# Scan of chunks 1 to 5 as one unit of four batches, with B and C turned on VectorE

## The chip, the core and the metric

The kernel runs on one core of one Trainium2 chip. The metric is the time of one execution on the device in microseconds (us), the median of three runs. PE is TensorE (matmuls), DVE VectorE, ACT ScalarE, POOL GpSimd, and SP SyncE, which issues all loads and stores here.

## The reference

A chunked state-space scan, then a gated feed-forward layer (FFN) over its result:

```python
# x (4, 8, 768, 32)   a (4, 8, 768)   B, C (4, 8, 768, 16): batch, head, token, ...
L = np.exp(cum[:, :, :, None] - cum[:, :, None, :]) * causal     # decays inside a chunk
M = np.einsum('bhin,bhjn->bhij', Cc, Bc) * L
y_intra = np.einsum('bhij,bhjd->bhid', M, xc)
y_inter = np.einsum('bhin,bhnd->bhid', Cc, state) * np.exp(cum)[:, :, :, None]
y[:, :, sl] = y_intra + y_inter
state = decay_full[:, :, None, None] * state + sum_over_j(B_j x_j decay_from_j)
...
x = y.transpose(0, 2, 1, 3).reshape(3072, 256)
out = (1 / (1 + np.exp(-(x @ w_gate))) * (x @ w_val)) @ w_out    # 256 -> 1536 -> 256
```

All in float32. The length of a chunk is free as long as the result is the same.

## The kernel before, in words

The kernel cuts the 768 tokens into six chunks of 128, each in two halves of 64. A chunk has four batches, so 512 rows of the FFN. The FFN of chunk k goes over twelve blocks f of 128 of the 1536 columns: a gate product `pg` and a value product `pv` each (L784, six matmuls, since an exact float32 product is made from a high and a low part of x and of w), sigmoid on ACT, the products h on DVE, ACT and POOL (L715 to L745), and then the projection `po` of each batch j = 0 to 3 over all f (L821, L822, and in chunk 0 L810). In chunk 0 the first six f are single products (L775). Chunk 0 has a scan of its own (FirstUnit). The scan of chunk c+1 is woven into the FFN of chunk c.

For chunks 1 to 5 a unit is one batch of one chunk, and two units make a pair. For one unit: `products` turns the loaded B and C (tokens on partitions) with two TensorE transposes `pt` (L393, L394); ACT copies the result to `bct` and masks C by group of heads (L404, L408). `multiply` makes C times B for a pair (L473). `decays` scans a into the decay matrix on DVE (L428) and makes `bd`, B times the last decay (L438); `before` makes `cd`, C times the running decay (L450). `results` is the rest of a pair: `weigh` (L487), `within` (L499 the part inside a chunk, L506 the state's increment), `ml` and the state in the middle of the chunk `sm` (L514, L541), `inter` (L550), the parts `xh` and `xl` of the result (L564, L570), and `state` makes `sn` (L460). So TensorE makes six visits to the scan per chunk (multiply, within, inter for two pairs) and four pairs of transposes.

The order of the instructions on each engine is set while the program is built, by a list scheduler. Each piece of work is a generator that yields one step after another:

```python
yield step("pe", 0.24 if c else 0.45, needs, [("tp", u)], **{hold: 1})
yield step("act", 0.9 if c else 1.1, [], [("bct", u)], **{hold: -1})
```

A step names the engine, a planned cost, what it needs and makes, and buffers that it takes or gives back. `run` picks, among the steps that could begin within 0.1 us of the first, the one whose task has the earliest due time; due times come from a formula by chunk (`unit`, L945), and the table `DUES` overrides them by task name. A planned time is only used to put the instructions in order. Loads are steps on "sp" with the planned cost of one issue and a planned time of transfer; SP issues its DMAs in that order, over eight lanes. Per chunk the loads are 8 of `ab` (L288, the decays, repeated over partitions from the scratch tensor `a_z`), 4 of `bn` and `cn` (L275), 2 of `xn` (L282) and 4 of `pp` (L296, from the scratch `a_p`). The two scratch tensors are written once (`save_z`, `save_p`, L895, L898) after `a` is clipped and its products are made (L883). A loaded weight tile is 512 KB; each of the 18 is clipped (L323), rounded and split into two parts over DVE, ACT and POOL (L330 to L353).

Of the kernel before, what the change touches and what calls it, by code (L numbers as in the profile page):

```python
# [37 lines left out]
LANES = 8  # L38
HOLD = 0.1
# [5 lines left out]
POOL_SB = 1.15  # L45
# [10 lines left out]
UNIT1_D = 7.0  # L56
FFN1 = 77.0
UNIT_T = 14.9
UNIT_D = 0.0
AHEAD = 46.7  # L60
STATE = 30.0
SPARE = 1.0
FILLS = {"products0_2": {0: 5}, "result0_1": {1: 2}, "result0_2": {1: 2}, "result0_3": {0: 3}}
# [6 lines left out]
def tile_ssd_then_gated_ffn(  # L70
# [25 lines left out]
    NDEC = 6  # L96
    NPRE = 5
# [82 lines left out]
    def run():  # L180
# [4 lines left out]
        landed = [0.0] * LANES  # L185

# [13 lines left out]
        while tasks:  # L200
# [30 lines left out]
            if eng == "sp":  # L231

                many, end = round(cost / 0.52), start
                for _ in range(many):
                    end = max(end, landed[-LANES]) + 0.52
                    dma_free = max(dma_free, end + DMA_L) + port / many
                    landed.append(dma_free + DMA_L)
            free[eng] = end
# [14 lines left out]
            try:  # L253
                t[2] = t[4].send(eng)
            except StopIteration:
# [8 lines left out]
    def pair_of(tag, c, b, shape):  # L264

        k = tag, c, b // 2
        if k not in got:
            got[k] = ld.tile([P, 2, H, shape], F32, tag=tag, name=f"{tag}{c}_{b // 2}", bufs=2)
        return got[k]

    def load_bc(c, b, n):
        cs = slice(c * L, (c + 1) * L)
        for tag, src in (("bn", b4), ("cn", c4)):
            t = pair_of(tag, c, b, N)
            nc.sync.dma_start(  # L275
                t[:, b % 2 : b % 2 + n].rearrange("p b h n -> p (b h) n"), src[cs, b * H : (b + n) * H]
            )

    def load_x(c, b, n):
        cs, hs, bs = slice(c * L, (c + 1) * L), slice(b * H, (b + n) * H), slice(b % 2, b % 2 + n)  # L280
        t = pair_of("xn", c, b, D)
        nc.sync.dma_start(t[:, bs].rearrange("p b h d -> p (b h) d"), x4[cs, hs])  # L282

    def load_a(c, b):
        t = ld.tile([P, H, L2], F32, tag="ab", name=f"ab{c}_{b}", bufs=NDEC)
        for i in range(2):
            src = a_z[2 * c + i, b * H : (b + 1) * H].rearrange("(o h) l -> o (h l)", o=1)
            nc.sync.dma_start(  # L288
                t[i * L2 : (i + 1) * L2].rearrange("p h l -> p (h l)"), src.broadcast_to([L2, H * L2])
            )  # L290
        got["a", c * NB + b] = t

    def load_p(c, b):
        t = ld.tile([P, L], F32, tag="pp", name=f"pp{c}_{b}", bufs=NPRE)
        src = a_p[b, :, c * L : (c + 1) * L].rearrange("h (o l) -> h o l", o=1).broadcast_to([H, N, L])
        nc.sync.dma_start(t, src)  # L296
        got["pp", c * NB + b] = t
# [18 lines left out]
    def split_w(i):  # L316
# [18 lines left out]
        yield step("pool", POOL_SB, [], [("whole", i)])  # L335
# [31 lines left out]
    units = {}  # L367
    states = {}

    def state_of(u, name):  # L370

        return wk.tile([P, NG * D], F32, tag=f"st{u % NB}", name=f"{name}{u}", bufs=3)

    class Unit:


        def __init__(self, c, b):
            self.c, self.b, self.u = c, b, c * NB + b
            self.nm = f"{c}_{b}"
            self.more = c < NCH - 1  # L380

        def products(self):

            c, b, u = self.c, self.b, self.u
            needs = [("bc", u)]
            if c:
                needs += [("bct", u - 1 if c > 1 else -1), ("cb", u - 4), ("cd", u - 4)]
            needs += [("x", 0, NB - 1)] if c == 1 else []
            pool, tag, hold = (ps_y, "py", "y") if c else (ps_mm, "mm", "banks")
            yield step("pe", 0.24 if c else 0.45, needs, [("tp", u)], **{hold: 1})  # L390
            bn, cn = (got[k, c, b // 2][:, b % 2].rearrange("p h n -> p (h n)") for k in ("bn", "cn"))
            pt = pool.tile([P, 512], F32, tag=tag, name=f"pt{self.nm}")
            nc.tensor.transpose(pt[:, :L], bn, eye)  # L393
            nc.tensor.transpose(pt[:, L : 2 * L], cn, eye)  # L394
            yield step("act", 0.9 if c else 1.1, [], [("bct", u)], **{hold: -1})
            if c:
                self.bct = wk.tile([P, 4, L], F32, tag="bct", name=f"bct{self.nm}", bufs=4)
            else:

                if ("bct", b // 2) not in got:  # L400
                    got["bct", b // 2] = hp.tile([P, 2, 4, L], F32, tag=f"h{b // 2}", name=f"bct{self.nm}")
                self.bct = got["bct", b // 2][:, b % 2]
            if c:
                nc.scalar.copy(self.bct[:, :2].rearrange("p k l -> p (k l)"), pt[:, : 2 * L])  # L404
            else:
                nc.scalar.copy(self.bct[:, 0], pt[:, :L])
            for g in range(NG):
                nc.scalar.mul(self.bct[:, 2 + g], pt[:, L : 2 * L], of_g[:, g : g + 1])  # L408
# [110 lines left out]
    def results(*two):  # L519
# [51 lines left out]
        if more:  # L571
# [3 lines left out]
            for k, t in enumerate(two):  # L575
                t.after = ml[:, k]
# [447 lines left out]
```

## Time and profile before

| what | value |
|---|---|
| the three runs | 378.0, 377.8, 377.15 us; median 377.8 us |
| span of the profiled execution | 375.7 us |
| its own time | not given apart; the runs lie 1.45 to 2.3 us above the span, the median 2.1 us |
| PE busy | 365.3 us, 97% of the span |
| DVE, ACT, POOL busy | 155.8, 151.2, 153.9 us, 41% each |
| the DMA engines | 26.27 MB, mean 70 GB/s |
| PE's last matmul ends | 372.4 us |

The span runs from the first to the last instruction of one execution. PE is the engine to follow: the others are busy for less than half the time, and what counts of them is when they make PE wait. "Granted clock" is the clock at which TensorE was allowed to run, 1.00 for 2.4 GHz and 0.50 for 1.2 GHz.

### The profile page before, as it was taken

What the parts mean: (1) busy time and instruction counts of PE and PEld (TensorE: products, weight loads), DVE (VectorE), ACT (ScalarE), POOL (GpSimd) and SP (SyncE); (2) the same over time, 40 slices, a digit from 0 to 9 for tenths busy, and PEclk for the clock granted to TensorE, in tenths of its full rate; (3) what the DMA queues carried; (4) which work ended last, traced back from release to release, by engine and by line L of the source; (5) the groups of instructions that cost most, each with busy time, mean ns of one, the idle gap of its engine ahead of it and who ended that gap; (6) DMA issues with size and microseconds to landing.
All of it is one profiled execution on the core that took longest, in us unless ns stands there. A gap on an engine that the chain in (4) does not pass through costs nothing.

```text
span 375.7 us, 8098 instructions
## 1 busy us (share of the span) xinstructions
PE 365.3 (97%) x3360; PEld 286.3 (76%) x3360; DVE 155.8 (41%) x280; ACT 151.2 (40%) x319; POOL 153.9 (41%) x161
## 2 busy tenths in 40 slices
PE   8879999989999999999999999999999999999996
PEld 2565478758788888887788888788877788888885
DVE  4774755854874234253431452550132440122201
ACT  2567578223536421436510435420335420244400
POOL 4346557573669540245430055430145420145410
PEclk9999999989999999999999999999999999999999
DMA  7998964087520043415502303120000000000000
GB/s 153 139 352 181 226 241 155 30 126 142 107 50 16 0 88 69 67 49 58 91 9 58 97 4 39 34 38 30 28 3 2 2 2 28 30 0 0 2 28 28
DMA packets 89270, 26.27 MB, mean 70 GB/s; under 512 B 76306, under 2 KB 82002, under 8 KB 89234
## 3 DMA queue, kind: packets, MB, share of 16 engines
q1 hardware_dynamic: 89234, 25.76, 30.7%
q8 instruction: 26, 0.43, 0.5%
q14 instruction: 10, 0.08, 0.1%
HBM read 22.41 MB, written 3.34 MB: 69 GB/s over the span
## 4 chain that ended last, share of the span: by engine, by line
PE 78%; SPq 12%; DMA 7%; issue 1%; DVE 1%; POOL 0%; DVEq 0%; POOLq 0%
PE pg L784 22%; PE pv L784 22%; PE po L821 15%; PE po L822 7%; SPq L275 4%; PE po L810 4%; DMA wr<-in_moe_w_gate_dram 3%; SPq L313 2%; PE pcb L499 2%; DMA a_z<-a 2%; SPq L309 2%; SPq L282 2%; SPq L288 2%; PE pcb L473 2%; DMA cn<-in_C_dram 2%; PE pcb L550 1%
## 5 line engine op out<-in xcount | busy, mean ns | idle before, releaser
L745 POOL TENSOR_TENSOR h<-g,h 128x512 fp32r<-128x512 f32 x60 | 79.0, 1316 | 124.6 <-ACT h L743 122.0
L784 PE MATMUL pg<-xh,w 128*128 128x512 f32 x264 | 93.8, 396 | 0.0
L784 PE MATMUL pv<-xh,w 128*128 128x512 f32 x264 | 93.7, 396 | 0.0
L821 PE MATMUL po<-w,h 128*128 128x512 f32 x228 | 81.8, 402 | 0.0
L739 DVE TENSOR_TENSOR g<-pv,g 128x512 f32<-128x512 f32 x60 | 41.4, 691 | 91.4 <-PE pv L784 86.6
L743 ACT CAST h<-g 128x512 fp32r<-128x512 f32 x60 | 37.3, 621 | 78.4 <-DVE g L739 78.4
L822 PE MATMUL po<-w,h 128*128 128x256 f32 x228 | 63.9, 280 | 0.0
L784 PEld LDWEIGHTS pg<-xh,w 128*128 128x128 f32 x264 | 49.5, 188 | 11.4 <-issue 0.5
L784 PEld LDWEIGHTS pv<-xh,w 128*128 128x128 f32 x264 | 49.6, 188 | 10.6 <-issue 0.2
L784 PE MATMUL pg<-xl,w 128*128 128x512 f32 x132 | 51.5, 390 | 0.0
L784 PE MATMUL pv<-xl,w 128*128 128x512 f32 x132 | 51.4, 390 | 0.0
L821 PEld LDWEIGHTS po<-w,h 128*128 128x128 f32 x228 | 42.8, 188 | 10.7 <-issue 0.2
L715 ACT ACTIVATE g<-pg 128x512 f32<-128x512 f32 x72 | 43.1, 599 | 19.4 <-PE pg L784 13.7
L822 PEld LDWEIGHTS po<-w,h 128*128 128x128 f32 x228 | 43.0, 189 | 0.2
L837 ACT COPY o<-po 128x256 f32<-128x256 f32 x20 | 7.5, 373 | 67.3 <-PE po L822 66.7
L839 DVE TENSOR_TENSOR o<-po,o 128x256 f32<-128x256 f32 x20 | 8.5, 425 | 59.8 <-ACT o L837 59.7
L353 POOL TENSOR_TENSOR w<-wr,w 128x512 fp32r<-128x512 f32 x18 | 24.7, 1371 | 14.2 <-ACT w L351 10.8
L428 DVE TENSOR_TENSOR_SCAN ab<-ab,delta 128x512 f32<-128x512 f32 x20 | 26.5, 1331 | 5.6 <-DMA ab<-a_z 5.6
L784 PEld LDWEIGHTS pv<-xl,w 128*128 128x128 f32 x132 | 24.8, 188 | 4.7
L784 PEld LDWEIGHTS pg<-xl,w 128*128 128x128 f32 x132 | 24.8, 188 | 4.6
L810 PE MATMUL po<-wr,h 128*128 128x256 f32 x96 | 24.9, 409 | 0.0
L336 POOL TENSOR_TENSOR wr<-wr 128x512 int32<-128x512 int32 x18 | 21.6, 1207 | 6.3 <-ACT wr L334 3.7
(106 smaller groups left out, 377.4 us busy)
## 6 DMA issues: line engine op xcount, KB each, us to landing
ab<-a_z SPq DMA_DIRECT2D x40, 128.0 KB
wr<-in_moe_w_gate_dram SPq DMA_DIRECT2D x6, 512.0 KB
wr<-in_moe_w_val_dram SPq DMA_DIRECT2D x6, 512.0 KB
wr<-in_moe_w_out_dram SPq DMA_DIRECT2D x6, 512.0 KB
out_dram<-o SPq DMA_DIRECT2D x24, 128.0 KB
xn<-in_x_dram SPq DMA_DIRECT2D x10, 256.0 KB
bn<-in_B_dram SPq DMA_DIRECT2D x10, 128.0 KB
cn<-in_C_dram SPq DMA_DIRECT2D x10, 128.0 KB
```

What stands on the lines that cost most here:

```text
L275: nc.sync.dma_start(t[:, b % 2 : b % 2 + n].rearrange("p b h n -> p (b h) n"), src[cs, b * H : (b + n) * H])
L336: nc.gpsimd.tensor_tensor(out=lw.bitcast(I32), in0=hw.bitcast(I32), in1=lw.bitcast(I32), op=ALU.add)
L353: engines[eng].tensor_tensor(out=lo, in0=lw, in1=hi.bitcast(F32), op=ALU.subtract)
L428: nc.vector.tensor_tensor_scan(out=t.rearrange("p h l -> p (h l)"), data0=t.rearrange("p h l -> p (h l)"), data1=delta.rearrange("p h l -> ...
L715: nc.scalar.activation(gs[k, f], pm, AF.Sigmoid)
L739: nc.vector.tensor_tensor(out=g, in0=pm, in1=g, op=ALU.mult)
L743: copies[eng](hh, g)
L745: engines[eng].tensor_tensor(out=hl, in0=g, in1=hh.bitcast(F32), op=ALU.subtract)
L784: nc.tensor.matmul(pm, w[:, part, kt, fs], xx[:, kt], start=(i == 0), stop=(i == 3 * NK - 1))
L810: nc.tensor.matmul(acc[:, :DM], hs[k, f][:, js], whole[NF + f // 2][:, f % 2], start=start, stop=stop, skip_group_check=True,)
L821: nc.tensor.matmul(acc, hh, w.rearrange("p i m -> p (i m)"), start=start, stop=False, skip_group_check=True)
L822: nc.tensor.matmul(acc[:, :DM], hl, w[:, 0, :], start=False, stop=stop, skip_group_check=True)
```

## The change

One class `Scan` does the scan of a whole chunk, four batches at once, for chunks 1 to 5.

- B and C come a second way: `load_rows` loads `bq` and `cq` with rows of 256 bytes (four tokens of one head), 16 DMAs of 32 KB per chunk, and `turned` transposes blocks of 32 by 32 on DVE (L399), eight instructions per chunk, straight into `bt` and `ct`. The TensorE transposes of chunks 1 to 5 and ACT's copies of them are gone; the masks `cg` are two ACT instructions of 128x512 (L412). `bn`, still needed for `bd`, is one load of 256 KB, `xn` one of 512 KB, `ab` two of 512 KB, `pp` four as before: 24 issues per chunk instead of 18.
- TensorE visits: `multiply` for four batches at once (L520), `within` in two visits of two batches with one step of rest between (L535, L542), `inter` for four batches (L484): four visits per chunk instead of six.
- `weigh` (L524) writes into `ab` in place, `before` (L433) into `ct` in place. The product of state and decay is an instruction of its own on POOL (`faded`, L438), made ahead of the sum. `xh`, `xl` are made in two steps of 128x512 (L495, L499).
- The planner gets a model of the DMA ring, other costs for POOL and for the two saves, and a much shorter table of due times; weights load in another order, with the rows of chunk 1 between them.

```diff
 DUES = {
...
+    "bn1": 101.7, "bq1_3": -90.9, "cq1_7": -1258.3, "state0_3": 121.3, "result0_2": 162.6, "w13": 131.8,
...
+    def load_rows(tag, c, src, bufs):
+        t = quad_of(tag, c, NG, NQ * N, bufs=bufs)
+        rows = src[:, :, c * L : (c + 1) * L].rearrange("b (q g) (t f) n -> b g q t (f n)", g=NG, f=NQ)
+        return [lambda b=b, g=g: nc.sync.dma_start(t[:, b, g], rows[b, g]) for b in range(NB) for g in range(NG)]
...
-            yield step("pe", 0.24 if c else 0.45, needs, [("tp", u)], **{hold: 1})
-            nc.tensor.transpose(pt[:, :L], bn, eye)
-            nc.tensor.transpose(pt[:, L : 2 * L], cn, eye)
...
+        def turned(self):
+            for tag, name, needs, makes in (
+                ("bq", "bt", [("cb", c - 1)], [("bt", c)]), ("cq", "ct", [("inter", c - 1)], [("ct", c)])
+            ):
+                yield step("dve", 1.1, needs + [(tag, c, i) for i in range(2 * NB)], makes)
+                t = wk.tile([P, NB, L], F32, tag=name, name=f"{name}{c}", bufs=1)
+                for b in range(NB):
+                    nc.vector.transpose(
+                        t[:, b].rearrange("p (t f) -> p f t", f=NQ),
+                        got[tag, c][:, b].rearrange("p g (f n) -> p f g n", f=NQ),
+                    )
+        def masked(self):
+            for g in range(NG):
+                yield step("act", 0.72, [("ct", c), ("cb", c - 1)], [("cg", c)] if g else [])
+                nc.scalar.mul(self.cg[:, :, g], self.ct, of_g[:, g : g + 1])
...
+        def before(self):
+            engines[eng].tensor_tensor(out=self.ct, in0=self.ct, in1=got["pp", c], op=ALU.mult)
...
+        def scan(self):
+            yield step("pe", 1.25, [("bt", c), ("cg", c)] + needs, [("cb", c)], cb=1)
+            for b in range(NB):
+                multiply(pcb[:, :, b * L : (b + 1) * L], self.bt[:, b], self.cg[:, b])
+            for b in range(NB):
+                yield step("dve", 0.7, [("cb", c), ("scan", c, b), ("bdec", c)], [("mult", c)])
+                weigh(dec[:, b], pcb[:, :, b * L : (b + 1) * L], dec[:, b])
+            for b in range(NB):
+                if b == 2:
+                    yield step("none", REST)
+                if b % 2 == 0:
+                    yield step("pe", 1.25, [("xn", c), ("mult", c), ("bdec", c)], [("y", c)] if b else [])
+                within(
...
+            nc.vector.tensor_tensor(out=self.s1, in0=self.sp, in1=ml, op=ALU.add)
+            yield step("pe", 1.25, [("cd", c)], [("inter", c)])
...
-        xs = [("xp", i) for i in range(2)] if k == 0 and not thin(k, f) else [("x", k, i) for i in range(NB)]
+        xs = [("xp", i) for i in range(2)] if k == 0 and not thin(k, f) else [("x", k, i) for i in range(NB)] if k == 0 else [("x", k)]
...
+    def loads_of(c):
+        block = [("pg", c - 1, 2)] if c > 1 else []
+            **some("a", 2, 1.4, [("y", max(c - 2, 0)), ("a_z",)], lambda: load_a(c)),
+            **some("bq", 2 * NB, 0.15, [("bt", c - 1)], lambda: load_rows("bq", c, Bm, 1)),
+            **some("cq", 2 * NB, 0.15, [("ct", c - 1), ("tp", NB - 1)], lambda: load_rows("cq", c, Cm, 1)),
+            f"bn{c}": load(1, 2.8, [("bdec", c - 2)] + block, [("bn", c)], lambda: load_tokens("bn", c, b4, N, 2)),
+            f"x{c}_": load(1, 3.3, [("y", c - 1)] + block, [("xn", c)], lambda: load_tokens("xn", c, x4, D, 1)),
+            **some("p", NB, 0.22, [("cd", c - 1), ("S", c - 1), ("a_p",)], lambda: load_p(c)),
```

What moves on the engines is shown at three places. First TensorE in the FFN of chunk 0, behind the last single value product (`pv_5`). Before (`pt` the transposes of unit after unit, `pg_6` and `pv_6` the products that follow):

```order
L775 MATMUL pv_5_608<-xw_256,wr_263 128x512 x2
L393 MATMUL pt_0_619<-eye,bn_0_523 128x128
L394 MATMUL pt_0_619<-eye,cn_0_525 128x128
L784 MATMUL pg_6_622<-xh_423,w_553 128x512
L784 MATMUL pg_6_622<-xl_424,w_553 128x512
L784 MATMUL pg_6_622<-xh_423,w_553 128x512 x2
L784 MATMUL pg_6_622<-xl_424,w_553 128x512
L784 MATMUL pg_6_622<-xh_423,w_553 128x512
L393 MATMUL pt_1_637<-eye,bn_0_523 128x128
L394 MATMUL pt_1_637<-eye,cn_0_525 128x128
```

With the change:

```order
L799 MATMUL pv_5_603<-xw_260,wr_360 128x512 x2
L520 MATMUL pcb_613<-cg_599,bt_577 64x128 x32
L808 MATMUL pg_6_657<-xh_357,w_564 128x512
L808 MATMUL pg_6_657<-xl_358,w_564 128x512
L808 MATMUL pg_6_657<-xh_357,w_564 128x512 x2
L808 MATMUL pg_6_657<-xl_358,w_564 128x512
```

The transposes between the products are gone, and chunk 1's whole multiply (`pcb`, 32 matmuls in the order) stands ahead of `pg_6`.

Second, TensorE late in the projection of chunk 0 (`po_0` to `po_2`). Before:

```order
L810 MATMUL po_2_868<-wr_567,h_6_662 128x256
L810 MATMUL po_2_868<-wr_567,h_7_705 128x256
L393 MATMUL pt_0_996<-eye,bn_0_890 128x128
L394 MATMUL pt_0_996<-eye,cn_0_892 128x128
L810 MATMUL po_0_846<-wr_540,h_8_755 128x256
L810 MATMUL po_0_846<-wr_540,h_9_789 128x256
L810 MATMUL po_0_846<-wr_461,h_10_826 128x256
L810 MATMUL po_0_846<-wr_461,h_11_853 128x256
L473 MATMUL pcb_1023<-bct_2_761 64x128 x8
L473 MATMUL pcb_1023<-bct_3_842 64x128 x8
L810 MATMUL po_1_858<-wr_540,h_8_755 128x256
```

With the change, where the first half of chunk 1's within stands (L535, L542):

```order
L834 MATMUL po_0_814<-wr_277,h_8_747 128x256
L834 MATMUL po_0_814<-wr_277,h_9_769 128x256
L834 MATMUL po_0_814<-wr_487,h_10_800 128x256
L834 MATMUL po_0_814<-wr_487,h_11_821 128x256
L535 MATMUL pcb_613<-ab_647,xn_558 32x64 x16
L542 MATMUL pcb_613<-xn_558,bd_851 32x64 x8
L535 MATMUL pcb_613<-ab_647,xn_558 32x64 x16
L542 MATMUL pcb_613<-xn_558,bd_851 32x64 x8
L834 MATMUL po_1_826<-wr_277,h_8_747 128x256
```

The transposes and the multiply of chunk 2 no longer stand in chunk 0's projection; the second half of within follows four matmuls of `po_1` later.

Third, SP's queue while the last weights are loaded. Before (`bn_0`, `cn_0` belong to chunk 1, `wr` are weights):

```order
L275 DMA bn_0_523<-in_B_dram 128x16x16
L275 DMA cn_0_525<-in_C_dram 128x16x16
L313 DMA wr_540<-in_moe_w_out_dram 128x2x512
L309 DMA wr_550<-in_moe_w_val_dram 128x2x512
L313 DMA wr_560<-in_moe_w_out_dram 128x2x512
L313 DMA wr_567<-in_moe_w_out_dram 128x2x512
L895 DMA a_z<-a_113 32x12x64
L898 DMA a_p<-a_114 32x768
L288 DMA ab_0_701<-a_z 64x512 x2
L288 DMA ab_0_716<-a_z 64x512 x2
```

With the change:

```order
L293 DMA bq_198<-in_B_dram 128x1x64 x3
L922 DMA a_p<-a_114 32x768
L293 DMA cq_344<-in_C_dram 128x1x64 x5
L293 DMA bq_198<-in_B_dram 128x1x64
L317 DMA wr_549<-in_moe_w_val_dram 128x2x512
L919 DMA a_z<-a_113 32x12x64
L287 DMA xn_558<-in_x_dram 128x32x32
L287 DMA bn_582<-in_B_dram 128x32x16
L299 DMA ab_647<-a_z 64x2048
L321 DMA wr_652<-in_moe_w_out_dram 128x2x512
L305 DMA pp_691<-a_p 128x1x128 x4
L299 DMA ab_647<-a_z 64x2048
```

The save of `a_p` stands ahead of the last six rows of `cq` and `bq` of chunk 1, and a weight behind them ahead of the save of `a_z`; `xn`, `bn` and the first `ab` of chunk 1 are ahead of the two last weights. On DVE the eight transposes of chunk 1 stand between two of the h products:

```order
L759 TENSOR_TENSOR h_3_573<-pv_3_543,g_3_561 128x512
L399 STREAM_TRANSPOSE bt_577<-bq_198 128x4x32 x4
L399 STREAM_TRANSPOSE ct_591<-cq_344 128x4x32 x4
L759 TENSOR_TENSOR h_4_601<-pv_4_570,g_4_596 128x512
L338 TENSOR_SCALAR wr_476<-wt_568 128x512
```

## Rows read from the trace of the kernel before

**Rows 1.** The page: span, PE's busy time, granted clock in 40 slices.
```profile
span 375.7 us, 8098 instructions
...
PE 365.3 (97%) x3360; PEld 286.3 (76%) x3360; DVE 155.8 (41%) x280; ACT 151.2 (40%) x319; POOL 153.9 (41%) x161
...
PEclk9999999989999999999999999999999999999999
```

**Rows 2.** Windows: length, busy PE, PEld, DVE, ACT, POOL, clock, DMA share, GB/s.
```profile
65.00:98.00 33.00, 30.45 (x423) 23.21 (x422) 19.40 (x32) 11.29 (x29) 19.44 (x22) 0.95 0.57 101
81.80:85.20 3.40, 3.40 (x31) 2.32 (x38) 0.00 (x0) 1.64 (x5) 2.11 (x3) 0.50 1.07 130
98.00:375.70 277.70, 274.40 (x2450) 225.44 (x2442) 97.12 (x167) 99.46 (x201) 98.03 (x93) 1.00 0.16 34
```

**Rows 3.** Waits of PE from 65 to 98 us: total, times, longest.
```profile
PE pt L394 <- DMA cn<-in_C_dram: 1.7, 1, 1.7
PE pcb L506 <- POOL bd L438: 0.7, 1, 0.7
PE pt L393 <- DMA bn<-in_B_dram: 0.2, 1, 0.2
```

**Rows 4.** Timeline of PE around 170 us: start, length, engine, line, operation.
```profile
161.34 0.39 PE L784 MATMUL pv<-xh,w 128*128 128x512 f32 x1
...
162.70 0.39 PE L784 MATMUL pg<-xh,w 128*128 128x512 f32 x1
...
172.38 0.27 PE L393 MATMUL pt<-eye,bn 128*128 128x128 f32 x1
...
173.98 0.39 PE L784 MATMUL pv<-xh,w 128*128 128x512 f32 x1
...
175.43 0.34 PE L550 MATMUL pcb<-cd,sn 32*64 32x64 f32 x8
...
176.06 0.50 PE L784 MATMUL pg<-xh,w 128*128 128x512 f32 x1
...
177.56 0.27 PE L393 MATMUL pt<-eye,bn 128*128 128x128 f32 x1
```

**Rows 5.** All instructions of line L393 on PE: durations, first and last start.
```profile
L393 PE MATMUL pt<-eye,bn x24: 270/272/331, 7.6 to 286.9; 128*128 128x128 f32 x24
```

**Rows 6.** Timeline of PE in the projection of chunk 0.
```profile
79.25 0.30 PE L393 MATMUL pt<-eye,bn 128*128 128x128 f32 x1 [0.21 <-DMA bn<-in_B_dram]
81.21 0.33 PE L394 MATMUL pt<-eye,cn 128*128 128x128 f32 x1 [1.67 <-DMA cn<-in_C_dram]
81.38 3.25 PE L810 MATMUL po<-wr,h 128*128 128x256 f32 x8
...
93.37 2.08 PE L810 MATMUL po<-wr,h 128*128 128x256 f32 x8
```

**Rows 7.** Timeline of DVE and PE while the weights are prepared.
```profile
34.60 0.69 DVE L735 TENSOR_TENSOR h<-pv,g 128x512 f32<-128x512 f32 x1 [2.30 <-POOL wr L336]
...
36.58 1.88 PE L775 MATMUL pg<-xw,wr 128*128 128x512 f32 x4
...
45.10 1.74 DVE L883 TENSOR_TENSOR_SCAN a<-a,a 32x768 f32<-32x768 f32 x1
...
46.88 0.27 PE L393 MATMUL pt<-eye,bn 128*128 128x128 f32 x1
```

**Rows 8.** Groups of DVE by form: count, busy, mean ns of one.
```profile
L739 DVE TENSOR_TENSOR g<-pv,g 128x512 f32<-128x512 f32 x60 | 41.4, 691 | 91.4 <-PE pv L784 86.6 <-PE pt L393 4.8
L428 DVE TENSOR_TENSOR_SCAN ab<-ab,delta 128x512 f32<-128x512 f32 x20 | 26.5, 1331 | 5.6 <-DMA ab<-a_z 5.6
...
L514 DVE TENSOR_TENSOR ml<-pcb,mask 128x128 f32<-128x128 f32 x10 | 2.9, 289 | 13.8 <-PE pcb L506 13.8
```

**Rows 9.** Timeline of SP's queue: start and length of an issue (x3: of three).
```profile
30.79 1.91 SPq L275 DMA_DIRECT2D cn<-in_C_dram  x1
...
58.46 1.90 SPq L296 DMA_DIRECT2D pp<-a_p  x3
...
132.07 0.37 SPq L275 DMA_DIRECT2D bn<-in_B_dram  x1
```

More of the change, by code (lines that the diff above doesn't have):

```diff
@@ L233, in run @@
                 many, end = round(cost / 0.52), start
+                size = HEAVY if port > 2.5 else LIGHT
                 for _ in range(many):
-                    end = max(end, landed[-LANES]) + 0.52
+                    end = max(end, landed[-LANES])
+                    while sum(d for at, d in ring if at > end) > RING - size:
+                        end = min(at for at, _ in ring if at > end)
+                    end += 0.55
                     dma_free = max(dma_free, end + DMA_L) + port / many
                     landed.append(dma_free + DMA_L)
+                    ring.append((dma_free, size))
+                del ring[:-20]
             free[eng] = end
@@ L279, in load_x @@
[L279 to L297, printed above, removed]
+    def load_bc(b):
+        for tag, src in (("bn", b4), ("cq", c4)):
+            t = quad_of(tag, 0, H, N, bufs=2 if tag == "bn" else 1)
+            nc.sync.dma_start(t[:, b], src[:L, b * H : (b + 1) * H])
+    def load_x(b):
+        nc.sync.dma_start(quad_of("xn", 0, H, D, bufs=1)[:, b], x4[:L, b * H : (b + 1) * H])
@@ L299, in tile_ssd_then_gated_ffn, with load_p @@
+    def load_p(c):
+        t = quad_of("pp", c, L, bufs=1)
+        src = a_p[:, :, c * L : (c + 1) * L].rearrange("b h (o l) -> b h o l", o=1)
+        return [lambda b=b: nc.sync.dma_start(t[:, b], src[b].broadcast_to([H, N, L])) for b in range(NB)]
     raws, wgv, wo = {}, {}, {}
@@ new lines, in before, with faded, early @@
+            engines[eng].tensor_tensor(out=self.ct, in0=self.ct, in1=got["pp", c], op=ALU.mult)
+        def faded(self, state, i):
+            t = wk.tile([P, NB, NG * D], F32, tag="sp", name=f"sp{self.c}", bufs=1)
+            nc.gpsimd.tensor_tensor(
+                out=t, in0=state,
+                in1=got["pp", self.c][:, :, i * L2 + L2 - 1 : (i + 1) * L2].broadcast_to([P, NB, NG * D]), op=ALU.mult,
+            )
+            return t
+        def early(self):
+            c = self.c
+            yield step("pool", 0.7, [("S", c - 1)] + [("p", c, b) for b in range(NB)], [("sp", c)], port=True)
+            self.sp = self.faded(states[c - 1], 0)
@@ new lines, in state, with multiply @@
+        def state(self):
+            c = self.c
+            yield step("pool", 0.7, [("inter", c)], [], port=True)
+            sp = self.faded(self.s1, 1)
+            eng = yield step(("dve", "pool"), (0.42, 0.7), [("after", c)], [("S", c)], port=True)
+            states[c] = state_of(c, "sn", 2)
+            engines[eng].tensor_tensor(out=states[c], in0=sp, in1=self.after, op=ALU.add)
+    def multiply(out, bt, cg):
+        for q in range(NQ):
+            qs = slice(32 * q, 32 * q + 32)
+            for i in range(2):
+                half = slice(i * L2, (i + 1) * L2)
+                nc.tensor.matmul(out[half, q], bt[qs, half], cg[qs, :, half], start=True, stop=True)
@@ L487, in weigh @@
+    def weigh(m, pcb, dec):
         nc.vector.tensor_tensor(
[L488 to L494 removed]
+            out=m.rearrange("p (q g) l -> p q g l", g=NG), in0=pcb.rearrange("p q (g l) -> p q g l", g=NG),
+            in1=dec.rearrange("p (q g) l -> p q g l", g=NG), op=ALU.mult,
+        )
@@ L495, in within @@
+    def within(m, xn, bd, out, local, first=True, more=True):
         for kt in range(NK):
@@ L728, in value @@
         if k == 0:
-            held = {5: [("S", u) for u in range(NB)], 8: [("p",)], 9: [("a_p",)], 10: [("a_z",)]}.get(f, [])
+            held = {5: [("S0", u) for u in range(NB)], 8: [("p",)], 9: [("a_p",)], 10: [("a_z",)]}.get(f, [])
             held += [("used", i) for i in range(NPLAIN)] + [("xp", 1)] if f == NF - 1 else []
@@ new lines, in chunk @@
+    def chunk(due, c):
+        s = Scan(c)
+        for k, g in loads_of(c).items():
+            task(due - AHEAD + LATER * (k[:2] in ("bn", "x%d" % c)), k, g)
+        task(due, f"turned{c}", s.turned())
+        task(due, f"masked{c}", s.masked())
+        task(due, f"before{c}", s.before())
+        task(due, f"decays{c}", s.decays())
+        task(due, f"early{c}", s.early())
+        task(due, f"scan{c}", s.scan())
+        if s.more:
+            task(due + STATE, f"state{c}", s.state())
@@ L979, in tile_ssd_then_gated_ffn @@
     for k in range(NCH):
-        for b in range(NB):
-            if k + 1 < NCH and k:
-                unit(t + UNIT_T + UNIT_D * b, k + 1, b)
+        if 0 < k < NCH - 1:
+            chunk(t + UNIT_T, k + 1)
         for f in range(NF):
```

423 lines of the change are left out of this document (182 added, 241 removed), and 24 rows, old and new, of the table DUES.

## The prediction

> **What bounds the kernel now.** I read the page first: TensorE is busy for 365.3 of 375.7 us [rows 1], so time is gained by giving it less to do or by removing its waits, and lost by new waits. Then the windows by stage: from 98 us to the end TensorE does not wait except for the last output, so there only work removed counts; between 65 and 98 us it is busy for 30.45 of 33.00 us at a mean clock of 0.95 [rows 2]. The waits of that stretch name its causes: the transposes of chunk 2 wait 1.7 and 0.2 us for their loads, and the increment of chunk 1 waits 0.7 us for `bd` on POOL [rows 3]. Behind the longest wait the granted clock is 0.50, that is 1.2 GHz, for 3.40 us [rows 2]. Last the timeline, for the price of a visit and of a pair of transposes.
>
> **1. Transposes off TensorE.** The trace has 24 of the first transposes; four are chunk 0's and stay, so 20 pairs go [rows 5]. Undisturbed, a product begins 1.36 us after the last (161.34 to 162.70); with a pair ahead, 172.38 to 173.98 is 1.60 [rows 4]. So a pair costs 0.24 us, and 20 give **-4.8 us**. The recorded lengths of 0.27 each overlap what follows and are not the price.
>
> **2. Fewer visits.** The product begun at 173.98 would end at 175.34; the inter begins at 175.43, 0.09 later. The product behind it takes from 176.06 to 177.56, 1.50 instead of 1.36, 0.14 more [rows 4]. A visit costs 0.23 us beyond its content, which stays. Chunks 1 to 5 have six visits before and four now, ten fewer in all: **-2.3 us**.
>
> **3. The stretch from 65 to 98 us.** Its idle time is 33.00 - 30.45 = 2.55 us, and 3.40 us at half the clock lose another 1.70: 4.25 us [rows 2]. In the new order no transpose or multiply of chunk 2 lies there, and the increment waits for a `bd` made in one instruction behind chunk 1's scans. What would be late next is chunk 1's `weigh`. I place the multiply at 47 us and within at about 77 us: 16.3 us of products (twelve at 1.36) and 28 projection steps at 0.46 (the undisturbed eight matmuls at 93.37 reach the next transposes in about 1.9 us, four steps [rows 6]) are 29 us, with the multiply itself 1.2. The four scans at 1.3 and four weighs near 0.69 [rows 8] are 8 us on DVE, between the conversions of the last weights; I put their end at 73 to 75 us, 2 to 4 us of slack. I take **-4.2 us**; the bounds are 0, if as long a wait and its clock return, and -4.25.
>
> **4. The start.** A weight needs DVE, ACT and POOL in turn, and the early h products stand in DVE's order between those steps; so the h at 34.60 followed a wait of 2.30 us for POOL, while its own products were done [rows 7]. By the new order, the clip of the 13th weight stands ahead of the second h, and I work out that weight's landing from the order at about 35.5 us. Then the fourth gate product starts between 36.6 and 37.2 instead of 36.58. I take **+0.3**; the bounds are -1.2 (the earlier loads of the first weights carry through) and the first rival.
>
> **5. Transposes on DVE.** No row shows one. The nearest, 128x128 from PSUM, is 0.29 us [rows 8]; I bound it by 0.2 below and by a scan's 1.33 above, and take 0.3, since shape and size are those of that row. Eight are 2.4 us per chunk on an engine that is busy for 97 of 278 us behind 98 us [rows 2]: cost nothing, as long as they end in time. In chunks 3 to 5, counted from the start of an FFN, I place them at 17 to 20 us, the two masks end at 22.3, and TensorE comes to the multiply after 17 products of 1.36, at 23.1: 0.8 us to spare. In chunk 1 the last rows land at about 42 us, after the save of `a_p`, and the masks end at about 45.5 against 46.9, when the single products end [rows 7]. The cover is 0.8 and 1.4 us.
>
> The Trainium skill ("VectorE: DVE Perf Modes", the rules for kernel authors) says that a 128×128 transpose belongs on TensorE where a PSUM destination is fine, and on DVE a transpose of 32×32 blocks is fastest. The first half speaks against the change, the second for it, since the rows of four tokens make the 32×32 blocks sufficient; no run here has shown which holds, and by the first half the -4.8 us would be missing and the time would be 371.6.
>
> **6. Everything else.** Inter's chain, `ml` at 0.29 us [rows 8] and one sum, has a product of 1.36 us or four projection steps ahead of inter to hide in. The 128x512 `xh` and `xl` of chunk 1 I place 0.6 to 0.9 us ahead of the next FFN. The last output is unchanged. All cost nothing as long as the 0.6 us hold. More issues on SP, 24 for 18 per chunk, have the FFN of a chunk (some 45 us) to hide in; by the rows an issue takes 0.37 to 0.63 us [rows 9], 9 to 15 us in all.
>
> **Sum.** -4.8 - 2.3 - 4.2 + 0.3 = -11.0 us on the span of 375.7: 364.7. The runs' median is 2.1 us over the span, so the time is **366.8 us**.
>
> **The rivals.**
> *A. The start pays.* If the fourth gate product comes more than a microsecond late, TensorE idles there and the clock falls as it did behind the wait at 81.21: the eight matmuls at 81.38 took until 84.56 instead of 1.9 us [rows 6], and the half clock cost 1.7 us in all. 0.7 to 2 us of wait and that give 2.4 to 3.7 more, less the 0.3 counted: 368.9 to 370.2. For it: the wait in rows 7 is of this kind, and weights are still landing. Against: the loads of x, B and C of chunk 1 that stood ahead of that weight (one of them held SP for 1.91 us [rows 9]) are mostly moved behind it.
> *B. Turning is dear.* At 0.6 us per transpose eight cost 2.4 us more. Chunk 1 exceeds its 1.4 us by 1.0, with the dropped clock 2.7; chunks 3 to 5 exceed their 0.8 by 1.6 at most, less where loads were early: some 1 us each. 366.8 + 2.7 + 3 = 372.5; at 0.45, about 369.
> *C. The small loads serialise, and it gets slower.* SP's queue also shows issues of 1.91 us [rows 9], when it was full. Chunks 2 to 5 load these 16 tiles of rows between the third gate product and the transposes. With `ab` ahead there are some 17 us for these, so a price of 1.1 us per load is where it begins to cost. At 1.3 us the wait is 3 us per chunk, 12 in all, and the gain is gone; at 1.5 us, 6 us per chunk, 24 in all: about 391. For it: sixteen transfers of 32 KB per chunk are new. Against: issues of the same queue took 0.37 and 0.63 us [rows 9], and in 98 us to the end the DMA engines were busy for a share of 0.16 [rows 2].
>
> The Trainium skill ("DMA: Bandwidth & Descriptors", anatomy of one DMA) gives a fixed 2.0 us per DMA plus its bytes, most of it the wait for the receipt, measured for the path of GpSimd. Were these paid one after the other, sixteen would be 33 us by that estimate, 16 late per chunk, and the time about 430 us. The issues of rows 9 lie closer than that, so here the fixed part overlaps.
>
> **How the numbers follow.** The forecast with its small slips (364.8 to 368.5) has 0.60; A 0.18; B 0.12, of which a third lies above 371.5; C 0.05; a start that gains a microsecond (365 and below) 0.05. The range is 364.5 to 371.5: it takes in the better start, A and most of B, and leaves out C, the far end of B and about 0.05 below. A measurement of this kernel can tell about 0.2% from no change, 0.8 us. Slower is C and a chunk 1 held up by the save of `a_p`, 0.05; within 0.2% takes a C or B that just eats the gain, 0.01; faster is 0.94.
>
> **What would show it.** Right: no TensorE transposes after 30 us; a busy PE without gaps and a clock of 1.00 from 65 us on; products 1.36 us apart where the pairs were; the second FFN beginning at 91 to 92 instead of 98 us. A shows as a gap of over a microsecond at the fourth gate product and a clock of 0.50 behind it; B as a wait of the multiply for ACT, with transposes over 0.45 us; C as a wait of DVE's transposes for `bq` or `cq` in every chunk. The prediction is wrong if the second FFN begins after 95 us, or if chunks 2 to 5 show waits of over 1 us each.

## The result and the profile after

The changed kernel takes 371.23 us (median of four runs, 369.5 to 372.75) against 377.48 before: ratio 0.984, 95% interval 0.9805 to 0.9875, a gain of some 6 us. Run again later (e0) it took 370.75 (370.11 to 371.05), ratio 0.9835 (0.9813 to 0.9856). The forecast was 366.8 in a range of 364.5 to 371.5, a gain of 11. The direction was right, and 4 to 5 us of the gain did not come; the range held, but narrowly, with the median 0.27 us inside its upper end and two of the four runs (371.83 and 372.75) beyond it.

The page of the changed kernel, to be read beside [rows 1]:

```profile
span 370.1 us, 7891 instructions
...
PE 357.8 (97%) x3320; PEld 283.5 (77%) x3320; DVE 159.1 (43%) x270; ACT 140.5 (38%) x259; POOL 157.5 (43%) x144
...
PEclk9989899999999999999999999999999999999999
```

TensorE has 7.5 us less to do (365.3 before), but the span is only 5.6 shorter: new waits ate the rest. The windows tell where (columns as in [rows 2]; first two of the kernel before, then three of the changed one):

```profile
27.00:47.00 20.00, 20.00 (x56) 10.39 (x56) 11.74 (x25) 13.48 (x24) 11.78 (x13) 1.00 0.96 209
47.00:65.00 18.00, 18.00 (x113) 14.51 (x112) 10.01 (x15) 13.86 (x33) 11.60 (x11) 1.00 0.59 199
```

```profile
27.00:47.00 20.00, 17.53 (x75) 9.18 (x60) 14.46 (x27) 12.21 (x22) 10.55 (x12) 0.91 0.78 225
47.00:65.00 18.00, 18.00 (x127) 12.62 (x126) 8.13 (x20) 11.65 (x20) 8.75 (x9) 1.00 1.17 189
65.00:98.00 33.00, 31.77 (x379) 25.41 (x378) 17.17 (x22) 12.51 (x24) 22.15 (x19) 1.00 0.07 21
```

From 27 to 47 us TensorE is idle for 2.5 us and its clock is at 0.91, where it had been full; the DMA engines are busy for 0.78 instead of 0.96 there and saturated afterwards. From 65 to 98 us the old waits and the half clock of [rows 2, 3] are gone, and one wait of 1.2 us has come. The waits of TensorE between 28 and 75 us (engine, line, what it waited for, total, times, longest):

```profile
PE pg L799 <- DVE h L759: 2.1, 1, 2.1
PE pv L808 <- POOL w L361: 1.2, 1, 1.2
PE pg L788 <- ACT xw L664: 0.4, 1, 0.4
```

and from 98 us to the end:

```profile
PE pcb L535 <- issue: 0.6, 1, 0.6
```

So behind 98 us one short wait is left, and the loss lies in the first FFN. TensorE's timeline there, beside [rows 7], whose fourth gate product began at 36.58 and whose first transpose behind the single products began at 46.88:

```profile
36.17 1.88 PE L799 MATMUL pv<-xw,wr 128*128 128x512 f32 x4
40.17 2.70 PE L799 MATMUL pg<-xw,wr 128*128 128x512 f32 x4 [2.12 <-DVE h L759]
42.67 2.91 PE L799 MATMUL pv<-xw,wr 128*128 128x512 f32 x4
...
52.37 1.21 PE L520 MATMUL pcb<-cg,bt 32*64 32x128 f32 x64
```

The fourth gate product waits 2.1 us, and the two products behind run at a lower clock (2.50 and 2.74 us from start to start instead of 1.72). DVE's timeline shows why the h was late:

```profile
34.76 1.74 DVE L907 TENSOR_TENSOR_SCAN a<-a,a 32x768 f32<-32x768 f32 x1
36.42 0.72 DVE L338 TENSOR_SCALAR wr<-wt 128x512 uint32<-128x512 uint32 x2
38.33 1.19 DVE L331 TENSOR_SCALAR wr<-wr 128x512 f32<-128x512 f32 x1 [1.19 <-DMA wr<-in_moe_w_gate_dram]
39.44 0.68 DVE L759 TENSOR_TENSOR h<-pv,g 128x512 f32<-128x512 f32 x1
```

The h at 39.44 is queued behind the scan of a and a clip that waits for its weight until 38.33. Whether it pays to move it is what e1 asks.

The profiled stretches of six runs, read from the first gate product of the second FFN, split the time in two:

| kernel | second FFN begins | last matmul ends | between |
|---|---|---|---|
| before | 98.03 | 372.40 | 274.4 |
| changed | 97.06 | 366.83 | 269.8 |
| changed, again (e0) | 95.66 | 365.11 | 269.5 |
| last clip later (f0) | 92.97 | 362.30 | 269.3 |
| pairs back (e4) | 97.32 | 371.57 | 274.3 |
| visits split (e5) | 96.33 | 368.30 | 272.0 |

In the three runs without added work the second part is 4.6 to 5.0 us shorter than before. Over all eleven profiles of the new order without added work it is 269.2 to 270.0 us, so most of what differs between them is decided in the first 98 us.

### The profile page after: what moved, and what is told of

Same layout as the page of the kernel before. It is cut to its first block, busy times and chain, and to the rows that moved or that the text cites. A ratio compares the mean times of both kernels' runs of the same rounds, so it can differ in the third digit from the quotient of the medians.

```text
span 370.1 us, 7891 instructions
## 1 busy us (share of the span) xinstructions
PE 357.8 (97%) x3320; PEld 283.5 (77%) x3320; DVE 159.1 (43%) x270; ACT 140.5 (38%) x259; POOL 157.5 (43%) x144
## 4 chain that ended last, share of the span: by engine, by line
PE 81%; DMA 7%; SPq 7%; DVE 2%; ACT 1%; issue 1%; POOL 1%; POOLq 0%; ACTq 0%
PE pv L808 23%; PE pg L808 22%; PE po L845 15%; PE po L846 7%; PE po L834 6%; DMA wr<-in_moe_w_out_dram 5%; DMA wr<-in_moe_w_gate_dram 2%; PE pcb L535 2%; SPq L280 2%; SPq L317 2%; PE pcb L484 1%; SPq L287 1%; PE pcb L520 1%; PE pcb L542 1%; SPq L299 1%
## 5 line engine op out<-in xcount | busy, mean ns | idle before, releaser
L769 POOL TENSOR_TENSOR h<-g,h 128x512 fp32r<-128x512 f32 x60 | 82.6, 1376 | 118.7 <-ACT h L767 118.6
L808 PE MATMUL pv<-xh,w 128*128 128x512 f32 x264 | 92.5, 391 | 1.2 <-POOL w L361 1.2
L808 PE MATMUL pg<-xh,w 128*128 128x512 f32 x264 | 92.4, 391 | 0.0
L767 ACT CAST h<-g 128x512 fp32r<-128x512 f32 x60 | 37.2, 620 | 79.0 <-DVE g L763 79.0
L420 DVE TENSOR_TENSOR_SCAN ab<-ab,delta 128x512 f32<-128x512 f32 x20 | 31.5, 1594 | 0.0
L361 POOL TENSOR_TENSOR w<-wr,w 128x512 fp32r<-128x512 f32 x18 | 23.8, 1328 | 12.9 <-ACT w L359 8.6
L344 POOL TENSOR_TENSOR wr<-wr 128x512 int32<-128x512 int32 x18 | 20.7, 1156 | 11.8 <-DVE wr L338 6.7
L834 PE MATMUL po<-wr,h 128*128 128x256 f32 x96 | 22.8, 392 | 0.0
```

Of the source, the lines that this page charges most:

```text
L344: nc.gpsimd.tensor_tensor(out=lw.bitcast(I32), in0=hw.bitcast(I32), in1=lw.bitcast(I32), op=ALU.add)
L361: engines[eng].tensor_tensor(out=lo, in0=lw, in1=hi.bitcast(F32), op=ALU.subtract)
L420: nc.vector.tensor_tensor_scan(out=t, data0=t, data1=delta.rearrange("p h l -> p (h l)"), initial=0.0, op0=ALU.mult, op1=ALU.add,)
L767: copies[eng](hh, g)
L769: engines[eng].tensor_tensor(out=hl, in0=g, in1=hh.bitcast(F32), op=ALU.subtract)
L808: nc.tensor.matmul(pm, w[:, part, kt, fs], xx[:, kt], start=(i == 0), stop=(i == 3 * NK - 1))
```

## The experiments

The runs write the planner's order of steps out as a list, which gives the changed kernel's instructions one by one; an edit is a move in that list. A line of the diffs below is one step: engine, then its name. Each ratio is to the kernel before on the same chip.

**Theories.** 1: the h of the second block is held by DVE's order, and what follows is passed on from it. 2: the first 70 us are paced by the last loads, and waits in front of them only shift. The rival to both: the weights' way through three engines paces the start, whatever the order.

**e0, the changed kernel again.** 

> The changed kernel unaltered, on the chip of the next three, as their yardstick. Both theories: 371 us, some 6 below the kernel before; a wait of about 2 us of TensorE at the fourth gate product for the h of the second block, the clock at half behind it, and a wait of about 1.2 us for POOL's split of a weight at 66 us.

370.75 us, ratio 0.9835. The waits differ from those of the first profile:

```profile
PE pv L808 <- POOL w L361: 2.6, 1, 2.6
PE pcb L520 <- ACT cg L412: 0.5, 1, 0.5
```

No wait for the h this time, but the multiply waits for the masks and begins at 49.42, and the wait for POOL is 2.6 us long. So the wait for the h is not the steady loss. Behind the wait for POOL stands POOL's own wait for the rows of a_p, as the first profile shows (in e0 it is 5.38 us):

```profile
64.99 1.29 POOL L433 TENSOR_TENSOR ct<-ct,pp 128x512 f32<-128x512 f32 x1 [4.34 <-DMA pp<-a_p]
66.23 1.48 POOL L361 TENSOR_TENSOR w<-wr,w 128x512 fp32r<-128x512 f32 x1
```

**e1, the h ahead.** 

> Only one instruction moves: on DVE the h of the second block stands ahead of the scan of a_p and of the clip of the weight of load 13 of 18, instead of behind both. Theory 1 (the h is held by DVE's order, not by its own inputs): the wait of 2.3 us and the half clock behind it (1.8 us) go; but the rows of B and C of chunk 1 arrive as late as before, the masks end near 50.4 us, and the multiply, which would now come at 48.3, waits for them about 2 us: about 2 us faster than the changed kernel, 369. Rival (the start is bound by the weights' way through DVE, ACT and POOL, whatever DVE's order): the wait turns up at the next product, the time stays within 1 us of the changed kernel's.

```diff
+dve value0_1 (h of the second block)
 dve ap (scan for a_p)
 dve split4, split5, split6 (the clip that waited)
-dve value0_1
```

370.08 us, ratio 0.9832 (0.98 to 0.9865), the same as e0. The wait is now one product further on:

```profile
PE pv L799 <- ACT g L739: 1.0, 1, 1.0
PE pv L808 <- POOL w L361: 0.9, 1, 0.9
```

Theory 1 is not borne out: with the h freed, the next product waits for the sigmoid on ACT. But e0, in which the h was not waited for, had nothing to free; what the edit is worth in an execution such as the first profile is not shown.

**e2, and the multiply later.** 

> As the run before, and on TensorE the multiply of chunk 1 stands behind the gate and value products of the seventh block instead of ahead of them. Theory 1: the masks are in time then, and the whole 4 us of wait and clock come back: about 367. If the masks were no obstacle, this equals the run before (within 0.7 us). Rival (weights bound the start): within 1 us of the changed kernel.

```diff
-pe scan1 (multiply)
 pe gate0_6, value0_6
+pe scan1 (multiply)
```

371.49 us, ratio 0.9843 (0.9816 to 0.987): no gain either, as the rival said.

**e3, POOL's decay product later.** 

> Only POOL's order changes: the product of C and the running decays of chunk 1 (L433), which waits 4.3 us for the loads of a_p's rows, stands behind the split of the last value weight instead of ahead of it. Theory 1 (TensorE's wait of 1.2 us at 66 us is that wait of POOL, passed on): it goes, and the time is 1.2 to 1.5 us less than the changed kernel's, near 369.8. Rival (that split is late by its own weight, which is loaded as the fourth from the end): no change.

```diff
-pool before1 (C with decays, L433)
 pool part11 (split of the last value weight, L361)
+pool before1
```

369.68 us, ratio 0.9808 (0.9784 to 0.9832), perhaps 1 us below e0, with overlapping intervals. The wait for POOL is gone, but another has come at the projection:

```profile
PE po L834 <- DVE h L759: 2.1, 1, 2.1
```

and DVE's timeline names its cause:

```profile
67.11 0.43 DVE L331 TENSOR_SCALAR wr<-wr 128x512 f32<-128x512 f32 x1 [3.26 <-DMA wr<-in_moe_w_out_dram]
...
67.79 1.22 DVE L420 TENSOR_TENSOR_SCAN ab<-ab,delta 128x512 f32<-128x512 f32 x1
68.92 0.67 DVE L759 TENSOR_TENSOR h<-pv,g 128x512 f32<-128x512 f32 x1
```

The clip of the last weight waits 3.26 us for its load and holds the scan and the h of the eleventh block. SP's queue of the changed kernel shows where the loads lost time:

```profile
36.18 3.50 SPq L293 DMA_DIRECT2D bq<-in_B_dram  x3
39.78 0.48 SPq L922 DMA_DIRECT2D a_p<-a  x1
40.30 3.49 SPq L293 DMA_DIRECT2D cq<-in_C_dram  x5
43.84 0.64 SPq L293 DMA_DIRECT2D bq<-in_B_dram  x1
...
46.20 4.26 SPq L287 DMA_DIRECT2D bn<-in_B_dram  x1
50.55 3.00 SPq L299 DMA_DIRECT2D ab<-a_z  x1
...
57.30 1.22 SPq L321 DMA_DIRECT2D wr<-in_moe_w_out_dram  x1
```

Nine loads of 32 KB and the save of a_p hold SP from 36.2 to 44.5 us, with the DMA engines busy for 0.58 of 35 to 45 us (1.00 before); then x, B and the decays come ahead of the last weight, issued at 57.30 to 58.52. The kernel before had its last weights issued by 46.85 and the decays after them.

**f0, the last clip and the first scan later.** 

> The run with the decay product of chunk 1 later, and on DVE the clip of the last weight and the first scan of chunk 1 stand behind the last two h of the first FFN instead of ahead of them (ACT's part of that weight moves with them). Theory 2 (the first 70 us are paced by the last loads, which come at 66 to 67 us; whatever DVE, POOL or TensorE does earlier only changes where the wait shows): the wait of 2.1 us of the projection for an h goes, about 367.6, unless the last weight itself is waited for in the projection's eleventh step. Rival, theory 1 (the start alone holds, the waits at 64 to 70 us are only passed on from it): no change against the run before it, 369.7.

```diff
-dve split15 (clip of the last weight), decays1 (first scan)
 dve value0_10, value0_11 (the last two h)
+dve split15, decays1
```

367.48 us, ratio 0.9742 (0.9718 to 0.9765): 2.5 us below e3, the run it adds to, and 3.5 us below e0, both with the intervals apart, at the place forecast. Its multiply begins at 49.52, as late as e0's, so the gain lies behind it. In its profile the trace names no wait of TensorE from 33 to 98 us, and the windows are all but full (columns as above):

```profile
47.00:65.00 18.00, 18.00 (x134) 13.69 (x133) 9.76 (x20) 12.61 (x22) 11.13 (x11) 1.00 1.13 176
65.00:98.00 33.00, 32.89 (x385) 26.39 (x384) 15.03 (x20) 12.98 (x26) 20.92 (x18) 1.00 0.13 37
```

Theory 2 holds for 60 to 72 us: instructions that waited for late loads stood ahead of what TensorE needed. What would be late next in f0 is chunk 1's weigh, which waits for `bd` on POOL and ends at 79.78, half a microsecond ahead of the within:

```profile
77.30 2.48 DVE L524 TENSOR_TENSOR ab<-pcb,ab 128x512 f32<-128x512 f32 x4 [0.99 <-POOL bd L425]
80.32 0.45 PE L535 MATMUL pcb<-ab,xn 64*32 64x64 f32 x32
```

**f1, the last weights ahead.** 

> The run before, and the loads of the last two weights are issued ahead of the save of a_z and of chunk 1's x, B and decays, instead of between and behind these; POOL makes chunk 1's bd, C with decays and faded state behind the weights. Nothing is computed otherwise. Theory 2 (the order of the loads, not their number, delays the weights): no wait left from 60 to 72 us, the second FFN begins near 93 us, the time is 366 to 367, and chunk 1's own loads, which come up to 3 us later, are still in time. Rival (the loads of chunk 1 are then the ones that are late): TensorE waits for weigh at the within of chunk 1, at about 79 us, and the gain is gone: 369 to 371.

```diff
+sp w13, w15
 sp save of a_z, xn, bn, ab
-sp w13
 sp pp, ab
-sp w15
-pool before1, early1
 pool split13, split14, split15, split17, split16, decays1
+pool before1, early1
```

369.43 us, ratio 0.9772 (0.9744 to 0.98), not faster than f0. The rival's wait is there, for weigh at the within of chunk 1:

```profile
PE pcb L535 <- DVE ab L524: 1.1, 1, 1.1
```

Its reason is another than the rival's: no engine waits for the loads that the edit puts back. The scans were done at 78.02, but `bd`, which this edit also moved, stood on POOL behind a weight's split, and weigh waited for it:

```profile
78.48 1.04 POOL L344 TENSOR_TENSOR wr<-wr 128x512 int32<-128x512 int32 x1 [2.66 <-DVE wr L338]
79.48 1.10 POOL L425 TENSOR_TENSOR bd<-bn,ab 128x512 f32<-128x512 f32 x1
80.61 2.48 DVE L524 TENSOR_TENSOR ab<-pcb,ab 128x512 f32<-128x512 f32 x4 [2.27 <-POOL bd L425]
```

In this profile 2.0 of the 2.8 us by which the second FFN begins later than in f0 stand already at the multiply (51.53 against 49.52), where the second gate product was late already (34.21 against 32.26, behind products at a granted clock of 0.50 from 27.46 to 34.21), ahead of the first load that the edit moves. So the run does not settle what the order of the loads alone is worth; with `bd` left where it was, and without f0's edit, it was not tried.

**e4, twenty pairs back.** 

> The changed kernel with twenty idle pairs of 128x128 TensorE transposes (of a constant, into a bank that nobody reads), four in each of the first five FFNs, between products. The price in the prediction, 0.24 us a pair: 4.8 us slower than the changed kernel, near 375.5. If the transposes' recorded 0.27 us each were their price: 10.8 us. If they hid beside the weights' loading: 0.

```diff
+            if token == "pair":
+                pt = ps_y.tile([P, 512], F32, tag="py", name=f"pair{len(pairs)}")
+                for h in range(2):
+                    nc.tensor.transpose(pt[:, h * L : (h + 1) * L], eye, eye)
```

376.15 us, ratio 0.9964 (0.9941 to 0.9986); against e0's 0.9835 that is 0.0129 of 377, 4.9 us give or take 1.2, or 0.24 a pair. The timeline shows one:

```profile
115.49 0.38 PE L203 MATMUL pair<-eye 128*128 128x128 f32 x2
115.62 0.48 PE L808 MATMUL pv<-xh,w 128*128 128x512 f32 x1
...
117.09 0.40 PE L808 MATMUL pg<-xh,w 128*128 128x512 f32 x1
```

From 115.49 to 117.09 is 1.60 us for a pair and a product, as in [rows 4]. In the table above the part behind the second FFN's begin is 4.8 us longer than e0's; sixteen pairs at 0.24 are 3.9 of it, and the other 0.9 stays open.

**e5, ten visits more.** 

> The changed kernel with the multiply and the inter of chunks 1 to 5 in two visits of two batches each, one product or a few projection steps between: ten visits more, no work more. The price in the prediction, 0.23 us a visit: 2.3 us slower, near 373. Rival (the visits are free, the content alone counts): no change.

```diff
             for b in range(NB):
+                if b == 2:
+                    yield step("pe", 0.6)
                 multiply(pcb[:, :, b * L : (b + 1) * L], self.bt[:, b], self.cg[:, b])
```

(and the same in inter). 375.55 us, ratio 0.9936 (0.9906 to 0.9966): 0.0101 of 377 above e0, 3.8 us (give or take 1.4) instead of 2.3. The profiled execution took 373.31, 2.2 us below that median. In the table above its part behind the second FFN's begin is 2.5 us longer than e0's, for eight visits, some 0.3 each, of which 0.2 in all is a wait for `xl`. What the slower executions add has no profile and stays open.

**g1, chunk 0's scan sooner.** 

> The run f0 (last clip later), and in chunk 0's own scan two instructions of DVE move: the half state of the third batch stands ahead of three clips of weights instead of behind them, and the wide increment of the fourth batch ahead of two. Theory 2: the start gains 1 to 2 us up to the first gate products, but chunk 1's last rows of B and C land at about 46 us as before, so that TensorE waits as much longer for the masks at the multiply: between no change and 1 us faster than f0, 366.5 to 367.5. Rival (the rows and masks have time to spare): the whole gain, near 366 or below.

```diff
+dve result0_2 (half state of the third batch)
 dve split7, split1, split3, state0_1
+dve result0_3 (wide increment of the fourth)
 dve split8
-dve result0_2, result0_3
```

368.48 us, ratio 0.9773 (0.9746 to 0.98), not faster than f0. The first value product (L788) now waits a microsecond itself, until 29.26, for nothing that the profile names, and the multiply begins at 50.22.

**g2, and e2's edits.** 

> The run before, and the h of the second block ahead of the scan of a_p and a clip, and the multiply of chunk 1 two products later on TensorE (both edits of the run e2). Theory 2: the masks are then covered and the start's gain arrives, 365.5 to 366.5, the best of all runs. Rival (the weights of the products behind pace TensorE): equal to the run before within 0.5 us.

369.52 us, ratio 0.98 (0.9774 to 0.9825). With the h ahead, the wait of 1.0 us for the sigmoid is back, as in e1; as in e1, the run without the edit had no wait for the h to free. The rival's equality with g1 within 0.5 us is not told apart from a loss of 1 us (0.98 against 0.9773).

**r1, the first loads as before.** 

> The run f0 (last clip later) with SP's first loads in the order of the kernel before: the first value weight ahead of B and C of the fourth batch, x of the first batch ahead of the second gate weight. Nothing else moves. If these two places make the start late (the single gate products from the second on begin at 31 to 33 us in the runs, at 29.71 in the kernel before): they begin 1 to 2 us sooner; the multiply of chunk 1 then waits up to 1.5 us for the masks, since the last rows land at 46 us, and the time is 366.5 to 367.5. Rival (the order of DVE and TensorE in chunk 0's scan makes it late): no change from f0, 367.5.

```diff
-sp w0
 sp x0
+sp w0
 sp b1, x2, x3, x1, b2
+sp w1
 sp b3
-sp w1
```

367.21 us, ratio 0.9745 (0.9732 to 0.9759), the same as f0: those two places are not the cause. The rival that this run leaves standing is the order of DVE and TensorE in chunk 0's scan.

**r2, and the multiply later.** 

> The run before with the multiply of chunk 1 two products later on TensorE. If the first loads make the start late and the masks would then be waited for: 365.5 to 366.5, below f0 by 1 to 2. Rival: within 0.5 us of f0.

367.64 us, ratio 0.9758 (0.9738 to 0.9779): no change either. The profiled execution, the slowest of the five (369.0), began early: its second gate product came at 30.62, and the fourth then waited for the h until 39.18:

```profile
39.18 1.99 PE L799 MATMUL pg<-xw,wr 128*128 128x512 f32 x4 [1.53 <-DVE h L759]
```

**What holds the start.** In the thirteen profiles of the new order the fourth gate product begins at 38.36 to 41.13 us; before it was 36.58. Two limits show. In nine profiles it comes 6.9 us behind the second gate product, without a wait, just as in the kernel before (29.71 to 36.58); there it is late because the second gate product is late, at 31.5 to 34.2. In the three in which the second gate product came first of all (30.55 in e3, 30.62 in r2, 31.02 in the first profile) it waited for the h, for 0.9 to 2.1 us. In e2 a lowered clock (0.72 from 33.49 to 36.00 us) stretches them. So an early start met the h, and a late one did not need it.

Of the late second gate product about a microsecond is seen in the rows. Before:

```profile
26.59 0.63 PE L634 MATMUL mm<-cd,wide 128*128 128x64 f32 x4 [0.75 <-DVE mr L514]
27.06 1.09 PE L764 MATMUL pv<-xw,wr 128*128 128x256 f32 x4
...
29.71 1.88 PE L775 MATMUL pg<-xw,wr 128*128 128x512 f32 x4
```

In e0:

```profile
27.76 1.14 PE L788 MATMUL pv<-xw,wr 128*128 128x256 f32 x4
28.74 0.55 PE L647 MATMUL mm<-cd,wide 128*128 128x64 f32 x4
29.65 1.14 PE L788 MATMUL pg<-xw,wr 128*128 128x256 f32 x4 [0.35 <-ACT xw L664]
...
31.49 1.88 PE L799 MATMUL pg<-xw,wr 128*128 128x512 f32 x4
...
38.36 1.99 PE L799 MATMUL pg<-xw,wr 128*128 128x512 f32 x4
```

Chunk 0's last visit (`mm`, L647) now stands behind the first value product instead of ahead of it, and the gate product behind it waits for ACT: from that value product to the second gate product it is 3.7 us instead of 2.65, in all profiles at the full clock. The rest varies from execution to execution; there is one profile of the kernel before, so how much its start varies is not known. No run moved that visit, and g1 moved only two instructions of DVE in chunk 0's scan. It was not tried either to load the projection's weights after those of the products (two of them now stand among the first nine loads, a third is the twelfth). What makes the start late is therefore shown in part only.

## Why the prediction was right in sign and too large

By its own sign the first FFN went wrong: it called itself wrong if the second FFN began after 95 us, and it began at 97.06, and at 95.66 in e0. Behind that the other signs came true: no TensorE transposes after 30 us, a clock of 1.00 from 65 us on, and no wait of over 0.6 us in chunks 2 to 5. By its own steps:

1. *Transposes off TensorE, -4.8 us.* Right. Put back, twenty pairs cost 4.9 us, give or take 1.2 (e4).
2. *Fewer visits, -2.3 us.* Right in kind, perhaps small: some 0.3 us a visit in the trace of e5 where the prediction had 0.23 from one visit.
3. *The stretch from 65 to 98 us, -4.2 us.* The waits for chunk 2's loads and for `bd` and the half clock are gone, as said. The step that failed is "what would be late next is chunk 1's weigh": late next were the split of the last value weight, behind POOL's wait for the rows of a_p, and behind it the h of the eleventh block, held by the clip of the last weight. They cost 1.2 us in the first profile, 2.6 in e0, and f0 (with e3's edit) won 3.5 us by moving what stood in their way. The prediction had followed chunk 1's path alone through the last loads; it did not ask what else waited on the same queues. Nor did weigh have the 2 to 4 us of slack that it was given: it ended at 79.8 in f0 instead of 73 to 75, and 0.5 us was left only because the within came at 80.3 instead of 77.
4. *The start, +0.3 us.* Too small, and in the first profile the largest miss. A fourth gate product at 36.6 to 37.2 takes the products ahead of it to begin as before, the second at 29.71; it came at 31.02 (changed) and 31.49 (e0), a term that the sum did not have. The landing of the weight in front of the second h was placed well: counted by the trace's packets of 2 KB, 256 to a weight, its last packet ended at 35.9 against the 35.5 worked out. But DVE, waiting for it, went on only at 38.33, 2.4 us later (34.7 and 37.28 in e0). The multiply began at 52.37 (changed) and 49.42 (e0) instead of 47, a miss of 2 to 5 us; the first of these is rival A as described, a wait with a lowered clock behind it, the second has neither.
5. *Transposes on DVE, free.* Right from chunk 2 on, though one takes 0.395 us, not 0.3:

```profile
L399 DVE STREAM_TRANSPOSE bt<-bq 128x128 f32<-128x128 f32 x20 | 5.7, 395 | 0.5 <-DMA bq<-in_B_dram 0.5
```

   In chunk 1 the cover of 1.4 us did not hold: the last rows, placed at 42 us, were waited for until 47.7 in the first profile and 46.7 in e0, and in e0 the multiply waited 0.5 us for the masks. The first half of the rule in the Trainium skill ("VectorE: DVE Perf Modes", rules for kernel authors), that a 128×128 transpose belongs on TensorE, would have kept the 4.9 us of e4 on the engine that sets the time; the second half, that DVE is fastest for 32×32 blocks, is what this layout uses. The 311 ns of the Trainium skill (the same page, the three transpose paths) are for bf16; in float32 these rows show 395.
6. *Rival C, the small loads.* Not from chunk 2 on, where no engine waits for them; the sixteen of a chunk take 11.7 to 12.4 us in chunks 3 to 5, 0.73 to 0.77 each, where rival C begins to cost at 1.1. At the start, in the place where nothing was to spare, nine of them and a save held SP for 8 us and the last weight came later.

The second part of the program came as worked out: from the second FFN's begin to the end of the span it was 273.0 us (e0 272.6), where the prediction's begin of 91 to 92 and end of 364.7 leave 273.2 from the middle. f0, without the waits at 60 to 72 us, runs at 367.48, near the 366.8 forecast. That is in part luck: its multiply begins 2.5 us later than forecast, and from there to the second FFN it needs 43.5 us where the prediction left 44.5, a difference that no run takes apart. The last term, 2.1 us from the span to the time, was read between two executions: in every run that lists both, the time is 1.7 to 1.9 us above that run's own span.

## What to carry to other kernels

Price what is taken off the bound engine from an undisturbed stretch; two such prices, 0.24 and 0.23 us, came out as 0.24 and some 0.3. When a change reorders loads at the start, follow every queue to its last entry, and look for instructions that wait for a late load and stand ahead of what the bound engine needs: moving them back won 3.5 us (e3 and f0), and issuing the last weights earlier on top of that won nothing more (f1). A wait seen in one profile of a start that varies from run to run is not yet the cause: e0 did not have it, and the runs that freed it gained nothing. Ask what begins late as well as what waits: most of the late products here had no wait in front of them.

## What the runs showed of the hardware

From chunk 2 on SP took a median of 0.54 us (`cq`) and 0.57 (`bq`), single ones up to 3.3, to issue a 32 KB load with rows of 256 bytes; loads of 512 KB took a median of 0.40 (`xn`) and 0.54 (`ab`). So sixteen small loads take the queue sixteen issues. At the start nine of them and a save held it for 8.3 us, while the DMA engines were busy for a share of 0.58 of 35 to 45 us. DVE went on 2.4 to 2.6 us after the last packet of a weight it waited for (35.9 and 38.33, 34.7 and 37.28 us). The two products behind a wait of 2.1 us took 2.50 and 2.74 us instead of 1.72, at a granted clock of 0.67 on the mean of 40.17 to 45.41 us. The start of one and the same kernel differs by 3 us between two executions (the multiply at 52.37 and 49.42), while the part behind the second FFN's begin repeats within 0.4 us.
